# Attention and two mixers on one core: pairs 2 and 3 load into the buffers of pairs 0 and 1

## The chip, the cores and the metric

One core of a Trainium2 chip runs the whole program in one launch. The metric is the device time of one execution, in microseconds (us), as the median of several runs. Lower is better.

## What is computed

Three blocks follow each other. The first is attention over four batches of eight heads, 576 positions and 64 values a head: a pooled part (queries, keys and values averaged over groups of four positions, full softmax over 144 positions, result repeated four times) plus a local part (softmax over keys at most three positions away).

```python
q_d, k_d, v_d = (t.reshape(B, H, S // 4, 4, D).mean(axis=3) for t in (q, k, v))
out_up = np.repeat(sm_attn(q_d, k_d, v_d), 4, axis=2)
mask = np.abs(pos[:, None] - pos[None, :]) < 4
out_local = softmax(where(mask, q @ k.T / sqrt(D), -1e9)) @ v
x = merge_heads(out_up + out_local)                       # 4 x 576 x 512
# mixer 1
u = x + (relu(x.T @ w_tok1) @ w_tok2).T
x = u + relu(u @ w_ch1) @ w_ch2
# mixer 2
theta = x @ w_theta
u = x + w_tok_r @ (x * cos(theta)) + w_tok_i @ (x * sin(theta))
out = u + relu(u @ w_ch)
```

## The kernel before, in words

The sixteen pairs of heads (four a batch) are numbered 0 to 15, and two pairs make a quad, numbered 0 to 7. The queries and keys of a pair come in one DMA of 128 x 1164 float32 (582 KB, a tile named qk). The work is cut into small steps, Python generators, each advanced by one `yield` at a time:

- `P<n>` (`load_pair`, L375) allocates the qk tile of pair n and issues its DMA on SP. `W<n>` (`load_values`, L382) issues four DMAs for the local values (vw), `V<Q>` (`pool_values`, L391) one DMA of 650 KB for the values of quad Q to be pooled (vd), and then three POOL additions (L398 to L404).
- `K<n>` (`pool_pair`, L413) adds groups of four positions of qk on VectorE (DVE) in two instructions (L421, L422). The two pairs of a quad share one tile qkd.
- `F<Q>` (`quad_front`, L425) is the pooled attention of a quad: scores sd (L434, L443), maxima mxd (L452, L460), exponentials pd on ScalarE (ACT, L468, L473), a transpose pdt (L477, L482), the product od (L493 to L500), its normalisation ods (L504 to L507), a store of ods to DRAM (L510, L511), and a load back as xu, each row repeated (L516, L519). SP waits for the store to land before it issues the load.
- `L<n>` (`pair_local`, L522) is the local attention of a pair: scores s (L530, L533; L315 are matmuls of zeros ahead of the first four pairs), mx and pbuf on DVE (L545, L546), an exponential (L553), a transpose pt (L558), a copy plt (L561, L562), the product o (L568), and x on DVE (L577 to L582).
- `A<n>` (`add_pooled`, L590) adds xu to x, `T`, `E`, `U` are the token mixing, and `G0` to `G6` convert the int64 words of w_tok1 and w_tok2 into two float32r parts each (`converted`, L166: two ACT instructions L199 and L201, three DVE L203 to L215, one POOL L219, then L221 and L223). Tiles named raw and ww belong to these.

A table of step names, `ORDER` (L33 to L84), sets in which order the steps are advanced, and so the order of the instructions on each engine's queue, up to the end of mixer 1. `tc.manual_schedule` (L1131) records that order as it stands; a wait on one instruction holds up all that is queued behind it on its engine. Behind the table, mixer 2 (`stage_z`, `stage_y`, `stage_out`) is put in order by the framework's own scheduler.

The qk tiles come from a pool with four rotating buffers (L377), so that the order of the `P` steps decides which buffer a pair gets: pairs 0, 1, 4, 2 take the four fresh ones, pair 3 takes that of pair 0 and pair 5 that of pair 1. A DMA into a used buffer waits on SP until the readers of the old contents (`K` on DVE, the L533 matmuls on PE) are done. Score and transpose tiles in PSUM come from another pool with two buffers in turn (`wide`, L293), so that each waits for the last reader of the one before last.

Of the kernel before, what the change touches and what calls it, by code (L numbers as in the profile page):

```python
# [12 lines left out]
F32 = mybir.dt.float32  # L13
# [17 lines left out]
FIRST = 1  # L31
ROWS = ((8, 9), (0, 2), (4, 6), (2, 3))
ORDER = """  # L33
G3 P0 G2 I*2 P1 G3 P4 G3 V0 P2 G3 K0 G3 G2 I G2 I L0*2 P3 K1 F0 W1 L0 F0 L1 L0 G3 F0 V0 L1*2 V0 L2 W0 G1 G0 G6 V1 G2
K2 V0 G2 F0 L1 F0 L2 K3 K4 L0 F0 L0 L2 L1 G2 F1 L2 L1 L0 F0 F1 G1*2 F1 V1 F0 P5 F0 W3 L0 F1 G5 G0 L1 G0 F1 K5 G6 F2 L1
G0 P6 W2 G5 G6 L3 V1 F2 V1 L3 G6 F2 F1 L3 G1 G4 F1 L2 P7 L5 L2 L5 F1 G1 L3 A0 V2 X0 A1 T0 L3 G1 L5 G0 L3 T0 G0 L2 G2
F1 G4 F2 G5 T0 K6 T0 V2 X2 L2 G6 W5 F2 K7 V2 L4*2 E0.0*2 T0 L4 V3 V2 A2 L3 E0.1 L5 G4 L4 W4 L5 G6 L5 G4 L3 X2 F3 G5 P8
P9 A3 G4 F2 G5 E0.1 T1 G4 G5 T0 F2 V3 L4 F3 F2 T0 L4 V3 X2 F3 L6 V3 L6 X7 T0 P11 L6 X2 X0 F3 K8 U0.0 L6 T0 X2 X0 U0.0
F3 L4 U0.0 V4 K9 F2 F3 X0 L6 L4 L6 T1 F4 U0.1 X0 F3 T1 L5 U0.1 X0 T1 U0.1 F4 X7 X4 V4 F3 T1 X7 F4 W6 L5 X7 E1.1 F4
E1.0 E1.1 L8 V4 L8 X7 E1.0 X1 A4 F4 T1 P10 A5 T1 X2 T2 L8 T1 U1.0*2 T2 T1 U1.0 X1 F3 L7 X7 L7 T2 X1 T2 X4 X5 K10 X1 L8  # L40
L6 U1.1*2 L7 T2 E2.0 U1.1 W7 X4 L7 V4 X1 L7 F4 W9 L7 L6 X4 E2.1 E2.0 C0 E2.1 T2 X1 L8 K11 X5 L7 T2 X5 L8 W8 L9*2 L7 X5
P13 T2 P12 L9 L10 C0 A6 F5 X4 C0 U2.0 L10 U2.0 X5 U2.0 C0 X3 F5 X6 F4 F5 C0 A7 F4 L10 T3 X4 F5 L9 V5 T3 H0.1 L8 U2.1
F5 T2 H0.1 H0.0 K12 T3 L9 U2.1 X5 C0 L9 U2.1 K13 F4 X6*2 L10 T3 X3 W13 H0.0 X6 H0.2 F6 E3.0*2 V5 P14 T3 F6 V5 H0.2 F6
C0 V6 V5 L8 X3 E3.1 L9 H0.3 F5 E3.1 X3 W10 L9 F6 X3 F5 L10 V6 A9 T3 F5 T3 V6 U3.0 L10 K14 T3 V6 U3.0 X6 U3.0 T3 H0.3
# [43 lines left out]
LOWER, WIDE = 2, 2  # L88
MIX = 384
NMIX = 6  # L90
WARM = [24] + [12] * 3 + [0] * 12
DEEP = [4, 4]

B, H, S, D = 4, 8, 576, 64
# [20 lines left out]
def kernel(  # L115
# [172 lines left out]
    sb1 = actx.enter_context(tc.tile_pool(name="a1", bufs=1))  # L288
    sb2 = actx.enter_context(tc.tile_pool(name="a2", bufs=2))
# [3 lines left out]
    def wide(name):  # L293
        return big.tile([128, 2, 512], F32, tag="big", name=name)
# [17 lines left out]
    def warm(out, k):  # L312

        for _ in range(k):
            pe.matmul(out, zero[:, 0:128], zero[:, 0 : out.shape[-1]], start=True, stop=True)  # L315
# [4 lines left out]
    def step(name, gen):  # L320
        gens[name] = gen
# [52 lines left out]

    def load_pair(n):  # L375
        b, p4 = divmod(n, 4)
        qk = sb2.tile([128, 2, S + 6], F32, tag="qk", name=f"qk_{b}_{p4}", bufs=4)  # L377
        sp.dma_start(qk, qkT[b, p4])
        loaded[n] = qk
        yield  # L380
# [141 lines left out]
    def pair_local(n):  # L522
# [4 lines left out]
        s = wide(f"s_{at}")  # L527
        warm(s[:, 0, 192:512], WARM[n])
        for j in range(2):
# [419 lines left out]
    def lazily(f):  # L949
        yield from f()  # L950
# [190 lines left out]
    sb1 = ctx.enter_context(tc.tile_pool(name="c1p", reuse_waits="tile", bufs=1))  # L1141
    sb2 = ctx.enter_context(tc.tile_pool(name="c2p", reuse_waits="tile", bufs=2))
# [93 lines left out]
    T0, T1 = slice(0, HALF), slice(HALF, S)  # L1236
# [221 lines left out]
```

## Time and profile before

| what | value |
| --- | --- |
| median of 3 runs | 679.75 us (679.57 to 682.46) |
| profiled execution, its own time | 679.18 us |
| span of that execution, first to last instruction | 677.4 us |
| PE busy in the span | 655.6 us (97%) |
| DVE busy in the span | 519.8 us (77%) |
| ACT busy in the span | 321.1 us (47%) |
| POOL busy in the span | 100.1 us (15%) |
| chain that ended last, by engine | PE 84%, DMA 5%, DVE 5%, SP's queue 2%, ACT 2%, issue 1% |

The span and the busy times come from one profiled execution, whose own time lies 0.57 us under the median of the runs. What lies around the span is 1.78 us. PE is the engine with the most work; the windows below show in which stretches it is idle.

### The profile page before, as it was taken

How to read it: one execution, taken by the hardware profiler on the slowest of the kernel's cores; microseconds unless marked ns; L12 is line 12 of the kernel's file. 1: busy time of each engine (PE TensorE's matmuls, PEld its weight loads, DVE VectorE, ACT ScalarE, POOL GpSimd, SP SyncE). 2: the span in 40 equal slices, each digit the busy share in tenths (PEclk: the TensorE clock that was granted, in tenths of full speed). 3: DMA queues.
4: the chain of work that ended last, by engine and by line, in shares of the span. 5: the costliest groups of instructions: out<-in, count | busy, mean ns of one | idle time of the engine just before them, and what ended most of it. 6: DMA issues, size and time to landing. Idle time of an engine off the chain costs nothing.

```text
span 677.4 us, 17394 instructions
## 1 busy us (share of the span) xinstructions
PE 655.6 (97%) x7320; PEld 625.6 (92%) x7320; DVE 519.8 (77%) x952; ACT 321.1 (47%) x632; POOL 100.1 (15%) x92
## 2 busy tenths in 40 slices
PE   7779889999999999999999999999999999999997
PEld 4658879989999999999999999999999998998997
DVE  5989988697542888998987867677898748847837
ACT  3566758355342564535434523154647227427311
POOL 3224222415000423300101200012000000000000
PEclk8889999999999999999999999999999999999999
DMA  8797877757343685527263762699510330140202
GB/s 294 235 300 236 269 248 250 254 184 233 105 147 126 221 294 187 202 65 214 57 195 128 206 142 85 236 323 277 141 63 0 106 121 1 62 142 1 71 1 70
DMA packets 93021, 109.93 MB, mean 162 GB/s; under 512 B 46880, under 2 KB 69536, under 8 KB 92944
## 3 DMA queue, kind: packets, MB, share of 16 engines
q1 hardware_dynamic: 92080, 106.08, 49.4%
q0 software_dynamic: 864, 2.75, 1.1%
q8 instruction: 57, 0.93, 0.6%
q14 instruction: 20, 0.16, 0.1%
HBM read 79.13 MB, written 29.69 MB: 161 GB/s over the span
## 4 chain that ended last, share of the span: by engine, by line
PE 84%; DMA 5%; DVE 5%; SPq 2%; ACT 2%; issue 1%; DVEq 0%; ACTq 0%
PE y L157 6%; PE y L158 6%; PE y L159 6%; PE c L158 4%; PE c L157 4%; PE c L159 4%; PE c L699 4%; PE c L702 4%; PE c L700 4%; PE c_p L902 3%; PE c_p L905 3%; PE c_p L903 3%; PE th L158 2%; PE th L159 2%; PE th L157 2%; DMA qk<-qkT 2%
## 5 line engine op out<-in xcount | busy, mean ns | idle before, releaser
L158 PE MATMUL y<-wrl,zh 128*128 128x288 f32 x256 | 74.9, 296 | 0.0
L157 PE MATMUL y<-wrh,zh 128*128 128x288 f32 x256 | 74.8, 296 | 0.0
L159 PE MATMUL y<-wrh,zl 128*128 128x288 f32 x256 | 71.9, 295 | 0.0
L219 POOL TENSOR_TENSOR ww<-ww,raw 128x512 int32<-128x512 int32 (+2 forms) x30 | 41.0, 1373 | 160.1 <-DMA raw<-w_ch 52.9
L157 PEld LDWEIGHTS y<-wrh,zh 128*128 128x128 f32 x256 | 48.0, 188 | 0.0
L158 PEld LDWEIGHTS y<-wrl,zh 128*128 128x128 f32 x256 | 48.0, 188 | 0.0
L159 PEld LDWEIGHTS y<-wrh,zl 128*128 128x128 f32 x256 | 46.9, 188 | 0.0
L219 POOL TENSOR_TENSOR raw<-raw 128x512 int32<-128x512 int32 (+2 forms) x16 | 20.4, 1275 | 133.5 <-DVE raw L215 57.6
L1231 DVE TENSOR_TENSOR cx<-y,cx 128x288 f32<-128x288 f32 x32 | 14.6, 456 | 32.3 <-PE y L159 31.8
L151 ACT CAST cuh<-cx 128x288 fp32r<-128x288 f32 (+1 forms) x16 | 8.8, 553 | 59.6 <-DVE cx L1231 59.6
L199 ACT ACTIVATE ww<-raw 128x512 f32<-128x512 f32 (+2 forms) x30 | 19.5, 649 | 27.4 <-DVE c1l L223 9.5
L157 PE MATMUL th<-thh,cxh 128*128 128x512 f32 (+1 forms) x92 | 31.6, 343 | 0.0
L158 PE MATMUL th<-thl,cxh 128*128 128x512 f32 (+1 forms) x92 | 31.6, 343 | 0.0
L159 PE MATMUL th<-thh,cxl 128*128 128x512 f32 (+1 forms) x92 | 31.1, 343 | 0.0
L921 DVE SCALAR_TENSOR_TENSOR g<-c,g 128x384 fp32r<-128x384 f32 x40 | 21.1, 549 | 12.8 <-ACT g L918 12.8
L918 ACT ACTIVATE g<-c 128x384 fp32r<-128x384 f32 x40 | 19.2, 490 | 24.4 <-PE c L159 24.4
L201 ACT ACTIVATE raw<-raw 128x512 int32<-128x512 uint32 (+3 forms) x46 | 29.5, 641 | 0.0
L929 DVE TENSOR_TENSOR ut<-c,ut 128x384 f32<-128x384 f32 x32 | 17.1, 550 | 9.9 <-PE c L702 9.9
L568 PE MATMUL o<-vw,plt 38*32 38x65 f32 x1280 | 18.0, 231 | 3.8 <-issue 3.1
L157 PE MATMUL t<-w2h,h 128*128 128x256 f32 (+1 forms) x64 | 21.5, 337 | 0.0
L157 PE MATMUL c<-uh,c1h 128*128 128x384 f32 x64 | 21.4, 334 | 0.0
L159 PE MATMUL c<-uh,c1l 128*128 128x384 f32 x64 | 21.4, 334 | 0.0
(390 smaller groups left out, 2256.7 us busy)
## 6 DMA issues: line engine op xcount, KB each, us to landing
raw<-w_ch SPq DMA_DIRECT2D x27, 512.0 KB
qk<-qkT SPq DMA_DIRECT2D x16, 582.0 KB
xT<-ut SPq DMA_DIRECT2D x12, 768.0 KB
vd<-vtok SPq DMA_DIRECT2D x8, 650.0 KB
vw<-vloc SPq DMA_DIRECT2D x32, 146.2 KB
uT<-us SPq DMA_DIRECT2D x16, 288.0 KB
ut<-uT SPq DMA_DIRECT2D x6, 768.0 KB
ut<-xT SPq DMA_DIRECT2D x6, 768.0 KB
```

The costliest lines, as they stand in the source:

```text
L157: pe.matmul(out, lh, rh, start=start, stop=False, skip_group_check=again)
L158: pe.matmul(out, lh, rl, start=False, stop=False, skip_group_check=again)
L159: pe.matmul(out, ll, rh, start=False, stop=stop, skip_group_check=again)
L201: act.activation(f, words[:, :, 0], AF.Copy, scale=2.0**-29)
L219: pool.tensor_tensor(out=w.bitcast(I32), in0=w.bitcast(I32), in1=f, op=ALU.add)
L699: pe.matmul(ps[:, 0:MIX], h[:, cb % 2, d], h1, start=cb == cbs[0], stop=False)
L700: pe.matmul(ps[:, 0:MIX], l[:, cb % 2, d], h1, start=False, stop=False)
L702: pe.matmul(ps[:, 0:MIX], weight[cb // 2][2][:, cb % 2, d], h2, start=False, stop=cb == cbs[-1])
L902: pe.matmul(ps[:, 0:MIX], h[:, cb % 2, d], h1, start=cb == cbs[0], stop=False)
L903: pe.matmul(ps[:, 0:MIX], l[:, cb % 2, d], h1, start=False, stop=False)
L905: pe.matmul(ps[:, 0:MIX], weight[cb // 2][2][:, cb % 2, d], h2, start=False, stop=cb == cbs[-1])
L921: dve.scalar_tensor_tensor(out=h2, in0=ps, scalar=0.0, in1=h1.bitcast(F32), op0=ALU.max, op1=ALU.subtract)
```

## The change

The qk tiles no longer rotate. A tuple `QK` names for each pair one of four buffers that are allocated apart, so that pairs 2 and 3 load into the buffers of pairs 0 and 1, and pairs 4 and 5 get the two fresh ones. `ORDER` is rewritten in its first eight lines: `P4`, `P5`, `K4`, `K5`, the front of quad 2 (`F2`) and the load of `V1` stand later, `W0` and two weight loads earlier. One line is added, so that all lines of the changed kernel behind L90 have a number one higher.

```diff
@@ -31,14 +31,14 @@
 ORDER = """
-G3 P0 G2 I*2 P1 G3 P4 G3 V0 P2 G3 K0 G3 G2 I G2 I L0*2 P3 K1 F0 W1 L0 F0 L1 L0 G3 F0 V0 L1*2 V0 L2 W0 G1 G0 G6 V1 G2
...
+G3 P0 G2 I*2 P1 G3*2 V0 G3 K0 G3 G2 I G2 I L0*2 P2 W0 G1 K1 F0 L0 F0 L1 L0 G3 F0 V0 L1 P3 G0 W1 L1 V0 L2 G2 K2 V0 G2
...
@@ -88,6 +88,7 @@
 LOWER, WIDE = 2, 2
 MIX = 384
 NMIX = 6
+QK = (0, 1, 0, 1, 2, 3, 0, 1, 3, 2, 3, 0, 2, 1, 3, 0)
 WARM = [24] + [12] * 3 + [0] * 12
 DEEP = [4, 4]
 
@@ -374,7 +375,7 @@
 
     def load_pair(n):
         b, p4 = divmod(n, 4)
-        qk = sb2.tile([128, 2, S + 6], F32, tag="qk", name=f"qk_{b}_{p4}", bufs=4)
+        qk = sb1.tile([128, 2, S + 6], F32, tag=f"qk{QK[n]}", name=f"qk_{b}_{p4}")
         sp.dma_start(qk, qkT[b, p4])
         loaded[n] = qk
         yield
```

**First place: SP's queue behind the load of pair 1.** Before, from that load on (qk_1, a name that drops the batch; the second qk row is pair 4, the third and fourth are pairs 2 and 3):

```order
L378 DMA qk_1_148<-qkT 128x1164
L378 DMA qk_0_152<-qkT 128x1164
L396 DMA vd_0_157<-vtok 128x1300
L378 DMA qk_2_159<-qkT 128x1164
L378 DMA qk_3_240<-qkT 128x1164
L387 DMA vw_1_266<-vloc 32x1170 x2
L387 DMA vw_1_266<-vloc 6x1170 x2
L387 DMA vw_0_364<-vloc 32x1170 x2
```

Now, from the same load on (the qk rows are pairs 1, 2 and 3):

```order
L379 DMA qk_1_148<-qkT 128x1164
L397 DMA vd_0_155<-vtok 128x1300
L379 DMA qk_2_236<-qkT 128x1164
L388 DMA vw_0_238<-vloc 32x1170 x2
L388 DMA vw_0_238<-vloc 6x1170 x2
L188 DMA raw_243<-w_tok 128x2x256
L379 DMA qk_3_342<-qkT 128x1164
L188 DMA raw_344<-w_tok 128x2x256
L388 DMA vw_1_346<-vloc 32x1170 x2
```

Pair 4 has left this place, the vw of pair 0 comes ahead of that of pair 1, and pairs 2 and 3, which now wait for the readers of pairs 0 and 1, stand ahead of vw and weight loads.

**Second place: SP's queue from the second vd to the vw of pair 3.** Before (the qk row is pair 5):

```order
L187 DMA raw_373<-w_tok 128x288
L396 DMA vd_1_375<-vtok 128x1300
L510 DMA od_0_57<-ods_0_567 4x32x256
L511 DMA ot_0_65<-ods_0_567 4x32x64
L378 DMA qk_1_589<-qkT 128x1164
L516 DMA xu_0_591<-od_0_57 128x1x1024
L519 DMA xu_0_591<-ot_0_65 64x1x256 x2
L387 DMA vw_3_595<-vloc 32x1170 x2
L387 DMA vw_3_595<-vloc 6x1170 x2
```

Now (the qk rows are pairs 4 and 5):

```order
L511 DMA od_0_57<-ods_0_557 4x32x256
L512 DMA ot_0_65<-ods_0_557 4x32x64
L397 DMA vd_1_578<-vtok 128x1300
L517 DMA xu_0_580<-od_0_57 128x1x1024
L520 DMA xu_0_580<-ot_0_65 64x1x256 x2
L379 DMA qk_0_585<-qkT 128x1164
L379 DMA qk_1_587<-qkT 128x1164
L188 DMA raw_589<-w_tok 128x288
L388 DMA vw_3_591<-vloc 32x1170 x2
L388 DMA vw_3_591<-vloc 6x1170 x2
L188 DMA raw_615<-w_tok 128x288
```

The vd of quad 1 has moved behind the store of quad 0 (od, ot), pairs 4 and 5 and one weight load behind the load of xu, and the vw of pair 3 and the last weight load behind all of these.

**Third place: DVE from the pooling of pair 5 to the maxima of pair 3.** Before (qa_1 is pair 5; the pooling of pair 4 stands 19 rows earlier, between those of pair 3 and mx_2):

```order
L421 TENSOR_TENSOR qa_1_670<-qk_1_589 128x576
L422 TENSOR_TENSOR qkd_0_446<-qa_1_670 128x288
L577 TENSOR_SCALAR rl_1_697<-o_1_623 128x10
L578 RECIPROCAL rl_1_697<-rl_1_697 128x10
L582 TENSOR_TENSOR x_0_603<-o_1_623,rl_1_697 128x2x5x64
L203 TENSOR_SCALAR ww_673<-ww_673 128x288
L206 TENSOR_SCALAR ww_673<-ww_673 128x288
L215 SCALAR_TENSOR_TENSOR ww_673<-raw_373,ww_673 128x288
L452 TENSOR_REDUCE mxd_0_732<-sd_0_676 128x4
L460 TENSOR_REDUCE mxd_0_732<-sd_0_676 64x1 x2
L545 TENSOR_REDUCE mx_3_816<-s_3_715 128x10
L546 TENSOR_TENSOR pbuf_120<-s_3_715,mx_3_816 128x2x5x38
```

Now (qa_0 and qa_1 are pairs 4 and 5):

```order
L578 TENSOR_SCALAR rl_1_669<-o_1_619 128x10
L579 RECIPROCAL rl_1_669<-rl_1_669 128x10
L583 TENSOR_TENSOR x_0_599<-o_1_619,rl_1_669 128x2x5x64
L422 TENSOR_TENSOR qa_0_674<-qk_0_585 128x576
L423 TENSOR_TENSOR qkd_0_673<-qa_0_674 128x288
L422 TENSOR_TENSOR qa_1_677<-qk_1_587 128x576
L423 TENSOR_TENSOR qkd_0_673<-qa_1_677 128x288
L204 TENSOR_SCALAR ww_666<-ww_666 128x288
L207 TENSOR_SCALAR ww_666<-ww_666 128x288
L216 SCALAR_TENSOR_TENSOR ww_666<-raw_589,ww_666 128x288
L546 TENSOR_REDUCE mx_3_783<-s_3_694 128x10
L547 TENSOR_TENSOR pbuf_120<-s_3_694,mx_3_783 128x2x5x38
```

The pooling of both pairs stands behind the x of pair 1 now, and the maxima of quad 2 (mxd_0) have left; they come after the xl of quad 0, with the six exponentials of that quad on ACT later in the same way. On PE the scores sd of quad 2 have moved from behind the o of pair 1 to behind the pt of pair 3.

Behind the table, in mixer 2, the framework's scheduler puts some matmuls of `stage_y`, and DVE and ACT instructions beside them, in another order than before. Their numbers and shapes are the same.

## Rows read from the trace of the kernel before

**Rows 1.** Windows of the whole core: us, busy per engine (count), granted clock, DMA.

```profile
0.00:50.00 50.00, 37.92 (x1045) 27.48 (x1045) 38.53 (x76) 26.90 (x67) 15.95 (x21) 0.90 0.84 277
50.00:100.00 50.00, 45.66 (x1410) 39.96 (x1409) 45.65 (x87) 32.86 (x75) 17.00 (x14) 1.00 0.80 253
100.00:150.00 50.00, 49.04 (x965) 44.73 (x966) 41.33 (x79) 29.47 (x71) 11.89 (x12) 1.00 0.68 226
...
500.00:550.00 50.00, 50.00 (x344) 48.08 (x343) 40.62 (x74) 22.88 (x38) 0.00 (x0) 1.00 0.28 94
```

**Rows 2.** PE's waits from 150 to 450 us: total, times, longest.

```profile
PE p_a L157 <- ACT p_p L866: 0.3, 1, 0.3
```

**Rows 3.** Chain of waits, first 50 us: start, us, what.

```profile
3.53 5.99 DMA qk<-qkT
...
23.12 3.81 DMA od<-ods
...
32.42 2.65 DMA raw<-w_tok
...
36.05 1.20 ACT pd L468 x4
...
45.41 1.26 PE pdt L477 x5
...
47.68 0.51 PE t L157
```

**Rows 4.** Timeline of SP: start, us, issue (the length holds its waits).

```profile
4.95 4.19 SPq L378 DMA_DIRECT2D qk<-qkT  x2
...
18.89 0.38 SPq L396 DMA_DIRECT2D vd<-vtok  x1
...
27.00 0.61 SPq L516 DMA_DIRECT2D xu<-od  x1
...
29.59 2.79 SPq L387 DMA_DIRECT2D vw<-vloc  x4
```

**Rows 5.** Windows of five us, columns as in the first group.

```profile
5.00:10.00 5.00, 2.69 (x110) 1.74 (x107) 3.29 (x7) 1.32 (x4) 0.80 (x1) 1.00 1.00 353
...
45.00:50.00 5.00, 5.00 (x61) 3.88 (x49) 4.71 (x8) 1.92 (x6) 2.81 (x3) 0.66 0.93 301
```

**Rows 6.** Timeline of PE: start, us, instruction, in brackets idle before and releaser.

```profile
14.98 0.91 PE L533 MATMUL s<-qk 64*32 64x38 f32 x80
...
29.00 1.60 PE L568 MATMUL o<-vw,plt 38*32 38x65 f32 x79
...
37.94 0.77 PE L558 MATMUL pt<-fixed,pbuf 128*128 128x128 f32 x5 [0.89 <-ACT pd L473]
```

**Rows 7.** Timeline of DVE, 18 to 44 us.

```profile
18.25 0.76 DVE L421 TENSOR_TENSOR qa<-qk 128x576 f32<-128x576 f32 x1
...
19.54 0.76 DVE L421 TENSOR_TENSOR qa<-qk 128x576 f32<-128x576 f32 x1
20.33 0.46 DVE L422 TENSOR_TENSOR qkd<-qa 128x288 f32<-128x288 f32 x1
...
23.83 0.76 DVE L452 TENSOR_REDUCE mxd<-sd 128x4 f32<-128x576 f32 x1 [0.73 <-PE sd L443]
...
30.30 1.44 DVE L422 TENSOR_TENSOR qkd<-qa 128x288 f32<-128x288 f32 x1
...
32.10 0.82 DVE L582 TENSOR_TENSOR x<-o,rl 128x640 f32<-128x640 f32 x1
...
36.42 0.55 DVE L546 TENSOR_TENSOR pbuf<-s,mx 128x380 f32<-128x380 f32 x1
...
41.94 1.48 DVE L606 TENSOR_TENSOR xl<-x,xh 128x1280 fp32r<-128x1280 f32 x1
```

**Rows 8.** Timeline of ACT at 35 us.

```profile
35.09 0.48 ACT L199 ACTIVATE ww<-raw 128x288 f32<-128x288 f32 x1 [4.25 <-DMA raw<-w_tok]
```

**Rows 9.** Timeline of POOL at 30 us.

```profile
29.73 1.69 POOL L219 TENSOR_TENSOR raw<-raw 128x512 int32<-128x512 int32 x1 [1.77 <-PE pdt L482]
```

More of the change, by code (lines that the diff above doesn't have):

```diff
@@ L33 @@
 ORDER = """
-G3 P0 G2 I*2 P1 G3 P4 G3 V0 P2 G3 K0 G3 G2 I G2 I L0*2 P3 K1 F0 W1 L0 F0 L1 L0 G3 F0 V0 L1*2 V0 L2 W0 G1 G0 G6 V1 G2
[L35 to L41, printed above, removed]
+G3 P0 G2 I*2 P1 G3*2 V0 G3 K0 G3 G2 I G2 I L0*2 P2 W0 G1 K1 F0 L0 F0 L1 L0 G3 F0 V0 L1 P3 G0 W1 L1 V0 L2 G2 K2 V0 G2
+F0 L1 F0 L2 K3 L0 F0 L0 L2 L1 G2 F1 L2 L1 L0 F0 F1 G1*2 F1 F0 V1 F0 V1 P4 P5 G6 W3 L0 F1 G5 G0 L1 G0 F1 G6 L1 K4 K5 G0
+P6 W2 G5 G6 L3 V1*2 L3 G6 F1 L3 G1 G4 F1 L2 P7 L5 L2 L5 F1 G1 L3 A0 V2 X0 A1 T0 L3 F2 G1 L5 G0 L3 T0 F2 G0 L2 G2 F1 G4
+F2 G5 T0 F2 K6 T0 V2 X2 L2 G6 W5 F2 K7 V2 L4*2 E0.0*2 T0 L4 V3 V2 A2 L3 E0.1 L5 G4 L4 W4 L5 G6 L5 G4 L3 X2 F3 G5 P8 P9
+A3 G4 F2 G5 E0.1 T1 G4 G5 T0 F2 V3 L4 F3 F2 T0 L4 V3 X2 F3 L6 V3 L6 X7 T0 P11 L6 X2 X0 F3 K8 U0.0 L6 T0 X2 X0 U0.0 F3
+L4 U0.0 V4 K9 F2 F3 X0 L6 L4 L6 T1 F4 U0.1 X0 F3 T1 L5 U0.1 X0 T1 U0.1 F4 X7 X4 V4 F3 T1 X7 F4 W6 L5 X7 E1.1 F4 E1.0
+E1.1 L8 V4 L8 X7 E1.0 X1 A4 F4 T1 P10 A5 T1 X2 T2 L8 T1 U1.0*2 T2 T1 U1.0 X1 F3 L7 X7 L7 T2 X1 T2 X4 X5 K10 X1 L8 L6
+U1.1*2 L7 T2 E2.0 U1.1 W7 X4 L7 V4 X1 L7 F4 W9 L7 L6 X4 E2.1 E2.0 C0 E2.1 T2 X1 L8 K11 X5 L7 T2 X5 L8 W8 L9*2 L7 X5
 P13 T2 P12 L9 L10 C0 A6 F5 X4 C0 U2.0 L10 U2.0 X5 U2.0 C0 X3 F5 X6 F4 F5 C0 A7 F4 L10 T3 X4 F5 L9 V5 T3 H0.1 L8 U2.1
```

## Prediction, made before the changed kernel was run

> **What bounds the kernel now.** I read the windows of the whole core first [rows 1]. In the first 50 us PE is busy for 37.92, in the next for 45.66, then 49.04, and from there on all of the time (the window from 500 us stands for it); between 150 and 450 us PE waits once, for 0.3 us [rows 2]. So an edit ahead of 150 us is worth what it takes from the 17.4 us of PE idle time there (12.1 + 4.3 + 1.0), and a delay that PE takes over is seen at the end in full. The chain of waits [rows 3] shows what ends last in the stretch of the change: the q and k of pair 1 (3.53 to 9.52 us), the round trip of od through DRAM (3.81), a weight load (2.65), and then the exponentials pd of quad 2, the transpose pdt and the first matmul t of the token mixing at 47.68. Between these it runs on DVE, whose timeline has hardly a gap there [rows 7]; the one of 0.73 us ahead of mxd is the only one in these rows. The reader should see in them that DVE pools pairs 3 and 4 (18.25, 19.54) without a wait: those loads are early. The timeline of SP [rows 4] shows the DMAs' places, the five-us windows [rows 5] the rate of the DMA engines when they are full, 353 GB/s, and the clock of 0.66 from 45 to 50 us, a mean of the two levels (1.2 and 2.4 GHz).
>
> **The price of a load.** I need it three times and the trace has it only for other places. The weight load (128 x 288 int64, 288 KB) took 2.65 us from issue to landing in a short queue [rows 3]; a qk (582 KB, 596,000 bytes) adds 0.85 us at 353 GB/s: 3.5 us. The other end is pair 1's 5.99 us in a full queue. I take 3.5 where the queue is short, which it is behind the moved loads.
>
> **The sum, step by step.**
>
> 1. *Pair 4 leaves the head of SP's queue.* vd and the vw are served some 1.7 us earlier (596,000 bytes at 353 GB/s). Nobody on the chain waits for them: 0.
>
> 2. *Pair 2 waits for pair 0's readers.* Pair 3 waited for the same readers before, and that issue ended at 9.14 [rows 4]. Landed by 12.6, at 5.99 by 15.1; DVE wants it at 17.0 (18.25 less the 1.25 of one pooling, below): 0 from both ends. The vw and weights queued behind it on SP were held up to 17 us and more before.
>
> 3. *Pair 3 waits for the scores of pair 1.* These end at 15.89 [rows 6], so it lands at 19.4 and DVE waits 1.15 us at 18.25 (at 5.99: 3.6). Pair 4's pooling, 19.54 to 20.79, is gone from here: -1.25. Together -0.1; I write 0. So od is issued at 23.1 as before (25.5 at the other end). mxd behind it had 0.73 us to spare [rows 7].
>
> 4. *od goes into an emptier queue.* Before, the vd issued at 18.89 and pair 5 lay around it. Now vd goes out behind od and pair 5 behind xu. Bounds 2.65 and 3.81; I take 2.65, as nothing large is ahead: xu is issued at 25.8, not at 27.0. The xu loads hold SP for 2.6 us (27.0 to 29.59 [rows 4]), up to 28.4; pairs 4, 5 and the weights take three issues of 0.38; vw comes at 29.6, as before: 0 for all behind. vd at 24.3 is landed by about 28.4 (3.5 and 0.2 for its larger size), and its first POOL addition ends some 2 us later, near where POOL had its next work (29.73 [rows 9]); od of quad 1 is wanted by DVE only behind pbuf of pair 3, at 37: 0.
>
> 5. *Pairs 4 and 5 are pooled behind x of pair 1.* The o of pair 1 ends at 30.60 [rows 6]. Its x ended at 32.92, 1.2 us behind a pooling that ended at 31.74 [rows 7]; with nothing in front it ends at 31.8. Pair 4, issued at 28.4, lands at 31.9 and is pooled to 33.15; pair 5 lands 1.7 us later, 33.6, and is pooled to 34.85; the weights land another 0.84 later, 34.4, and ACT's 0.48 us [rows 8] make them ready at 34.9. Three DVE instructions of this conversion (some 1.2 us), then mx and pbuf (1.15, at 0.55 us and a step between): pbuf of pair 3 ends at 37.25, where it ended at 36.97 [rows 7]: **+0.3**, although the maxima of quad 2 no longer stand there.
>
> One row needs a choice here. Pair 5's second instruction took 1.44 us, pair 4's 0.46 [rows 7], and beside the long one POOL ran an addition of 1.69 us [rows 9]. I take 0.46, since POOL's next additions should be over by 33.6. The Trainium skill, SBUF — State Buffer, section Who interferes with whom, says that a VectorE instruction with two SBUF inputs contends with a GpSimd instruction that reads SBUF; the two rows agree. By that rule 0.46 holds if POOL is quiet then; were the 1.44 the instruction's own, 1 us would be added.
>
> 6. *The front of quad 2 goes behind pt of pair 3.* Before, pt of pair 2 waited 0.89 us for pd [rows 6], and pd for an ACT queue that stood for 4.25 us on the weight load [rows 8]. Both waits leave pt. plt behind it still waits for that last weight load on ACT. This load is issued when it was, but behind pair 5, weights and vw, and lands at about 36.3 (34.4, 1.0 for 355,000 bytes of vw, 0.84), not at 35.07; two ACT instructions later plt starts at 37.2, where it started at 38.7 at the earliest (37.94 + 0.77). So ACT and PE are 1.5 us early, DVE 0.3 late, and xl of quad 0 ends between 0.5 earlier and 0.3 later than 43.42 [rows 7]. Now the maxima of quad 2 come behind xl: 0.76 and two of some 0.3, to 44.3 or 45.1. Then pd: 1.9 us from 36.05 to the pt that it released at 37.94 [rows 3, 6], and 0.2 ahead for scaling: 46.4 or 47.2. pdt took 2.27 us (45.41 to 47.68 [rows 3]) in the slow stretch; at the full clock I estimate 1.2. The first matmul of the token mixing starts between 47.6 and 49.5, against 47.68: **0 to +1.8**, middle +0.9.
>
> 7. *Up to the end.* DVE has 4.35 us and PE 4.34 us idle from 50 to 100 us [rows 1], mostly waits for each other, so I let half of the 0.9 be absorbed: **+0.5**. In mixer 2 the scheduler's other order costs 0 as long as PE has no wait, which the window from 500 us shows. If it opens a gap, I bound it by 1 us, two of DVE's short instructions (0.55) per batch in one batch.
>
> The profiled execution took 679.18 us, so the sum is 679.7; against the median of 679.75 it is 680.25. I forecast **680.0 us: no change**. About 0.5% (3.4 us) is what a measurement of this kernel can tell from no change.
>
> **Rivals.**
>
> *Slower: the loads that were early collide.* Some 1.5 MB (pairs 4 and 5, weights) leave the quiet stretch around 18 us for the one behind xu, where vd, xu, two qk, weights and vw queue up in turn. If pairs 4 and 5 pay 5.99 us instead of 3.5, all of step 5 is 2.5 us later: pbuf at 39.75, +2.8. Quad 2's maxima, 1.4 us, stay behind it, and the PE that stands idle meanwhile runs pdt at the low clock: +4.2 at the token mixing, some 684 us at the end. It decides from the point at which DVE starts on pair 5 later than about 35.5. For it: the DMA engines' share is 0.84 over the first 50 us [rows 1], and 0.93 from 45 to 50 [rows 5]. Against it: the emptier queue before 23 us, which lets od, vd and xu through early. The Trainium skill, DMA: Bandwidth & Descriptors, section Rules for kernel authors, says to issue a DMA early, compute, and wait late; by it this rival would be the result, and the absence of a wait ahead of pairs 3 and 4 in rows 7 bears it out as far as the kernel before goes. 13%.
>
> *Faster: the waits on ACT were the bound.* Then pt and plt, 1.5 us early, pull the rest along, the wait of 0.89 us is gone for good and pdt runs at the full clock (1.1 us): 3.5 us in all, 676.2. For it: PE's 12.1 us of idle time in the first 50 us. Against it: DVE runs through, and gets none of its work taken away, only moved. 9%.
>
> *The moves cancel* (no landing is late, quad 2's maxima delay nothing): -0.5 to +0.5 us, 679.5. That is inside my forecast's band.
>
> **Chances and range.** My forecast with the last case has 78%, faster 9%, slower 13%. Within the forecast the bounds are -1.0 (od and the landings at their short ends, full clock) and +2.4 (step 3 at 5.99 us, no absorption). For 8 in 10 the range reaches a little into both rivals: 677.3 to 682.9.
>
> **What would show it.** Right: DVE waits about a us ahead of pair 3's pooling at 19.4; xu is issued near 26; pairs 4 and 5 are pooled between 32 and 35 with 0.46 us for the second instruction; pt of pair 2 shows no wait for pd; the first t matmul stands at 47.6 to 49.5; PE runs through from 150 us. Wrong: DVE waits 2 us or more for pair 4 or 5 (slower), the t matmul starts before 46 (faster), or PE has waits in mixer 2.

## The result and the profile after

| | median | runs | lowest to highest |
| --- | --- | --- | --- |
| before | 680.96 us | 13 | 675.66 to 683.92 |
| after | 684.82 us | 13 | 683.32 to 689.59 |

The ratio is 1.007 [1.0047 to 1.0092]: the changed kernel is slower by 0.7%, some 4.8 us by the ratio (the medians differ by 3.9). The forecast of 680.0 us (677.3 to 682.9) and of no change was wrong; the time is that of the rival to which I had given 13%, some 684 us.

The profiled execution of after took 689.59 us, the slowest of its 13; that of before, 679.18, lies under its median. The two spans, 687.8 and 677.4 us, thus differ by 10.4, more than twice what the ratio says. PE is busy for 659.4 us of the new span: 3.8 more than the 655.6 before, for the same instructions, and idle for 28.4 where it was idle for 21.8. Nearly all of these 6.6 us lie in the first 150 us (16.0 + 5.0 + 2.8 = 23.8 idle, 17.4 before [rows 1]). Windows of after, columns as in [rows 1]:

```profile
0.00:50.00 50.00, 34.02 (x1007) 25.03 (x1008) 34.29 (x69) 25.61 (x63) 14.30 (x20) 0.85 0.82 262
50.00:100.00 50.00, 45.05 (x1222) 39.27 (x1221) 47.16 (x88) 32.23 (x75) 16.32 (x15) 0.94 0.71 225
100.00:150.00 50.00, 47.17 (x999) 43.02 (x987) 35.55 (x66) 25.59 (x59) 11.50 (x12) 0.93 0.73 239
500.00:550.00 50.00, 50.00 (x344) 48.10 (x343) 44.00 (x78) 26.19 (x46) 0.00 (x0) 1.00 0.15 47
...
20.00:25.00 5.00, 2.95 (x137) 2.34 (x125) 3.96 (x12) 2.49 (x6) 0.00 (x0) 1.00 0.10 26
25.00:30.00 5.00, 2.93 (x103) 2.28 (x104) 4.38 (x11) 4.22 (x11) 1.14 (x1) 0.84 0.81 278
30.00:35.00 5.00, 5.00 (x153) 3.55 (x152) 2.20 (x4) 0.00 (x0) 3.15 (x4) 0.81 0.98 343
35.00:40.00 5.00, 0.75 (x7) 0.35 (x5) 3.58 (x10) 2.27 (x6) 1.26 (x2) 0.87 1.05 276
40.00:45.00 5.00, 3.60 (x121) 2.83 (x123) 4.87 (x7) 3.79 (x8) 0.79 (x1) 0.50 0.98 281
45.00:50.00 5.00, 2.60 (x100) 2.31 (x89) 4.31 (x8) 4.18 (x13) 1.82 (x2) 0.50 0.92 325
50.00:55.00 5.00, 5.00 (x36) 4.14 (x34) 4.48 (x8) 1.57 (x4) 0.99 (x2) 0.50 0.94 268
```

The row to start from is the one at 20 us: the DMA engines are busy for 0.10 of it. The same window of before:

```profile
20.00:25.00 5.00, 3.98 (x121) 3.15 (x122) 4.02 (x11) 3.14 (x7) 0.00 (x0) 1.00 0.87 310
```

That is 1.55 MB moved before (5 us at 310 GB/s) and 0.13 MB now. The 1.4 MB come back from 30 us on, where the share is 0.92 and more. Behind them DVE and ACT have gaps, PE has 0.75 us of work from 35 to 40, and from 40 to 55 us it is granted 0.50, the lower of its two levels. The timeline of SP of after:

```profile
13.48 0.36 SPq L379 DMA_DIRECT2D qk<-qkT  x1
...
24.18 0.44 SPq L397 DMA_DIRECT2D vd<-vtok  x1
26.75 0.60 SPq L517 DMA_DIRECT2D xu<-od  x1
...
28.72 1.06 SPq L379 DMA_DIRECT2D qk<-qkT  x2
29.82 0.43 SPq L188 DMA_DIRECT2D raw<-w_tok  x1
```

And the timelines of DVE, ACT and PE of after, with the idle time before an instruction and its releaser in brackets:

```profile
19.28 0.78 DVE L422 TENSOR_TENSOR qa<-qk 128x576 f32<-128x576 f32 x1 [3.49 <-DMA qk<-qkT]
...
33.52 0.76 DVE L422 TENSOR_TENSOR qa<-qk 128x576 f32<-128x576 f32 x1 [2.50 <-DMA qk<-qkT]
34.32 0.46 DVE L423 TENSOR_TENSOR qkd<-qa 128x288 f32<-128x288 f32 x1
35.60 0.76 DVE L422 TENSOR_TENSOR qa<-qk 128x576 f32<-128x576 f32 x1 [0.83 <-DMA qk<-qkT]
36.40 0.46 DVE L423 TENSOR_TENSOR qkd<-qa 128x288 f32<-128x288 f32 x1
37.46 0.31 DVE L204 TENSOR_SCALAR ww<-ww 128x288 f32<-128x288 f32 x1 [0.60 <-ACT ww L200]
...
39.10 0.55 DVE L547 TENSOR_TENSOR pbuf<-s,mx 128x380 f32<-128x380 f32 x1
```

```profile
36.97 0.46 ACT L200 ACTIVATE ww<-raw 128x288 f32<-128x288 f32 x1 [7.53 <-DMA raw<-w_tok]
...
38.55 0.46 ACT L200 ACTIVATE ww<-raw 128x288 f32<-128x288 f32 x1 [0.77 <-DMA raw<-w_tok]
...
39.27 0.57 ACT L562 COPY plt<-pt 128x512 f32<-128x512 f32 x1
```

```profile
34.70 0.77 PE L559 MATMUL pt<-fixed,pbuf 128*128 128x128 f32 x5
...
39.72 0.50 PE L531 MATMUL s<-fixed,id 128*128 128x190 bf16 x2 [4.25 <-DVE pbuf L547]
...
51.65 0.58 PE L158 MATMUL t<-xh,w1h 128*128 128x256 f32 x1
```

Read from the top: pair 4 is awaited for 2.50 us and pair 5, 2.08 us behind it, for 0.83 more; the weight issued behind them lands last of the three, and ACT stands on it for 7.53 us. The pbuf of pair 3 ends at 39.65 (36.97 before [rows 7]); PE has waited 4.25 us for it. The first t matmul of the token mixing starts 4.0 us late (51.65, in the chain 51.72; before 47.68 [rows 3]). The chain that ended last shows the lengths of these loads in after:

```profile
13.48 5.71 DMA qk<-qkT
...
22.88 3.85 DMA od<-ods
...
29.82 7.13 DMA raw<-w_tok
...
49.38 1.33 PE pdt L478 x5
...
51.72 0.51 PE t L158
```

### The profile page after: what moved, and what is told of

It is laid out like the page before. It is cut to its first block, busy times and chain, and to the rows that moved or that the text cites. A ratio compares the mean times of both kernels' runs of the same rounds, so it can differ in the third digit from the quotient of the medians.

```text
span 687.8 us, 17391 instructions
## 1 busy us (share of the span) xinstructions
PE 659.4 (96%) x7320; PEld 629.8 (92%) x7320; DVE 521.5 (76%) x952; ACT 321.1 (47%) x632; POOL 98.5 (14%) x92
## 4 chain that ended last, share of the span: by engine, by line
PE 84%; DMA 7%; DVE 5%; ACT 2%; SPq 1%; issue 1%; DVEq 0%; ACTq 0%
PE y L159 6%; PE y L158 6%; PE y L160 6%; PE c L158 4%; PE c L160 4%; PE c L159 4%; PE c L700 4%; PE c L703 4%; PE c L701 4%; PE c_p L906 3%; PE c_p L904 3%; PE c_p L903 3%; PE th L158 2%; PE th L160 2%; PE th L159 2%; PE t L158 2%
## 5 line engine op out<-in xcount | busy, mean ns | idle before, releaser
L200 ACT ACTIVATE ww<-raw 128x512 f32<-128x512 f32 (+2 forms) x30 | 19.4, 646 | 31.1 <-DVE c1l L224 9.4
L159 PE MATMUL c<-ul,c1h 128*128 128x384 f32 x64 | 21.4, 334 | 0.0
```

What stands on the lines that cost most here:

```text
L159: pe.matmul(out, lh, rl, start=False, stop=False, skip_group_check=again)
```

## The experiments

All ratios are to the kernel before, run on the same chip beside it, with the 95% interval; before's median lay between 680.96 and 683.4 us from set to set, so that ratios are compared, not times. The edits move tokens in `ORDER`; the diffs show the pieces of its lines that differ. Nothing of the computation is left out.

### Undoing parts of the change

My theory after the result: the loads of pairs 4 and 5 are late, so issuing them early again, with all else as changed, gives the time back. The rival: the late front of quad 2 costs.

Both loads early, into their fresh buffers, behind the vw of pair 1:

```diff
-W0 G1 K1 F0 L0 F0 L1 L0 G3 F0 V0 L1 P3 G0 W1 L1
+W0 G1 K1 F0 L0 F0 L1 L0 G3 F0 V0 L1 P3 G0 W1 P4 P5 L1
...
-F0 V1 F0 V1 P4 P5 G6 W3
+F0 V1 F0 V1 G6 W3
```

> The changed kernel with the loads of pairs 4 and 5 issued ahead of the store of quad 0 (behind the vw of pair 1, near 17 us) instead of behind xu; SP's order alone changes. Theory of late loads: what the change lost is that two qk and a weight load queue up behind xu (DVE stood 2.50 + 0.83 + 0.60 us for them). Then these 3.9 us go: pbuf of pair 3 ends near 36 instead of 39.65 us, the first t matmul stands near 48 instead of 51.7, and the ratio to the kernel before is 0.998 to 1.002 (679.5 to 682.3 us). Theory of the late front: the maxima and exponentials of quad 2 behind xl are what PE waits for; then t comes at 50 us or later and the ratio stays at 1.005 or more (684 us).

Front of quad 2 at its old place, behind the pooling of pair 5:

```diff
-L1 K4 K5 G0
+L1 K4 K5 F2 G0
...
-L3 V1*2 L3 G6 F1
+L3 V1 F2 V1 L3 G6 F2 F1
```

> The changed kernel with the front of quad 2 back at its old place (scores behind the pooling of pair 5, maxima and exponentials ahead of those of pair 3); the loads stay late. Theory of late loads: the waits of DVE for pairs 4 and 5 and for the weight stay (3 to 4 us in all), 1.4 us of maxima come on top of them ahead of pbuf of pair 3 (near 41 us), and are gone from behind xl; t matmul at 49.5 to 52, ratio 1.004 to 1.009. Theory of the late front: t matmul at 48, ratio 0.998 to 1.002.

Both edits at once (no other line differs):

> The changed kernel with both: loads of pairs 4 and 5 early and the front of quad 2 at its old place. What is left of the change is the wait of pair 3 for the buffer of pair 1, vd of quad 1 behind the store of quad 0, and the order of the weight loads. Both theories: 0.997 to 1.002 and t matmul near 48 us. If it stays at 1.004 or more, the loss lies in what is left: pair 3 (DVE waits 3.5 us for it) or vd.

The front alone, late in the kernel before (`F2` moved as in the change):

```diff
-K5 G6 F2 L1
+K5 G6 L1
...
-L3 V1 F2 V1 L3 G6 F2 F1
+L3 V1*2 L3 G6 F1
...
-T0 L3 G1 L5 G0 L3 T0 G0
+T0 L3 F2 G1 L5 G0 L3 T0 F2 G0
...
-G5 T0 K6
+G5 T0 F2 K6
```

> The kernel before with the front of quad 2 alone moved as the change does (scores behind pt of pair 3, maxima behind xl, exponentials behind these); all loads as before. Theory of late loads: the move of the front costs little: pbuf of pair 3 some 1.4 us earlier (35.6 us), t matmul at 46.5 to 48.5, ratio 0.997 to 1.002. Theory of the late front: t matmul at 50 us or later, ratio 1.004 to 1.008.

| kernel | ratio |
| --- | --- |
| e1, loads of 4 and 5 early | 1.0051 [1.0023 to 1.0078] |
| e2, front early | 1.0111 [1.0065 to 1.0157] |
| e3, both | 1.0057 [1.0030 to 1.0084] |
| e4, before with the front late | 1.0003 [0.9974 to 1.0032] |

The rival is out: a late front costs nothing that these runs can tell, and with late loads an early one is not better but, by the middles, worse (e2). But e1 gives back only 0.2% by its middle; the theory as I stated it fell too. Its profile shows the two waits gone, and others in their place. The window at 20 us, DVE and ACT of e1:

```profile
20.00:25.00 5.00, 2.79 (x112) 2.22 (x102) 3.99 (x9) 2.52 (x7) 0.00 (x0) 1.00 1.03 293
...
20.01 0.76 DVE L422 TENSOR_TENSOR qa<-qk 128x576 f32<-128x576 f32 x1 [3.82 <-DMA qk<-qkT]
...
32.80 0.75 DVE L422 TENSOR_TENSOR qa<-qk 128x576 f32<-128x576 f32 x1
...
34.51 1.06 DVE L422 TENSOR_TENSOR qa<-qk 128x576 f32<-128x576 f32 x1
...
37.66 0.55 DVE L547 TENSOR_TENSOR pbuf<-s,mx 128x380 f32<-128x380 f32 x1
42.58 0.56 DVE L547 TENSOR_TENSOR pbuf<-s,mx 128x380 f32<-128x380 f32 x1 [0.74 <-ACT w1h L222]
...
35.49 0.49 ACT L200 ACTIVATE ww<-raw 128x288 f32<-128x288 f32 x1 [4.33 <-DMA raw<-w_tok]
```

Pairs 4 and 5 are there in time, the first weight behind xu still is not: ACT stands for 4.33 us on it, and DVE waits for ACT at 42.58. The length of that wait alone is not the loss, since ACT stood for 4.25 us on a weight in the kernel before, too [rows 8]. And the DMA engines are full from 20 to 25 us here (1.03), so that the idle window of after is gone without the loss being gone.

### One part at a time, in either kernel

Open now: the late pair 3 (3.5 us of waiting), the late vd, or the buffers. e5 takes e1 and gives pairs 2 and 3 fresh buffers, issued early; pairs 4 and 5 then go into those of pairs 0 and 1:

```diff
-QK = (0, 1, 0, 1, 2, 3, 0, 1, 3, 2, 3, 0, 2, 1, 3, 0)
+QK = (0, 1, 2, 3, 0, 1, 2, 3, 1, 0, 1, 2, 0, 3, 1, 2)
...
+V0 P2 P3 G3 K0
```

> The run with early loads (e1_loads_early) with pairs 2 and 3 in the two fresh buffers and issued right behind the first vd, and pairs 4 and 5 in the buffers of pairs 0 and 1; SP's order and the buffers change, the order of the compute engines does not. Theory of the late pair 3: in e1_loads_early DVE stood 3.82 us for pair 3 (issue 13.89, landed 20.0) and that wait is what is left of the loss, 0.5%. Then the wait is under 0.5 us, od of quad 0 is issued 2 to 3 us earlier (near 21 us), and the ratio is 0.998 to 1.002. Theory that the loss lies elsewhere (vd of quad 1, pooling of pair 4 taken out of the early part of DVE, buffers of later pairs): 1.004 to 1.007 in spite of it.

Before with the tuple of buffers written out, pairs and order as they were:

```diff
+QK = (0, 1, 3, 0, 2, 1, 3, 0, 1, 2, 1, 3, 2, 0, 1, 3)
...
-        qk = sb2.tile([128, 2, S + 6], F32, tag="qk", name=f"qk_{b}_{p4}", bufs=4)
+        qk = sb1.tile([128, 2, S + 6], F32, tag=f"qk{QK[n]}", name=f"qk_{b}_{p4}")
```

> The kernel before with the buffers of pairs 6 to 15 chosen as the changed kernel chooses them (pair 6 takes that of pair 2, 7 that of 3, 8 of 5, 9 of 4 and so on); the order of all engines stays. If the waits of the later loads for other readers are part of the loss: ratio 1.003 to 1.006, and PE loses its time behind 60 us, not ahead of it. If not: 0.998 to 1.002.

Before with the vd of quad 1 behind the store of od:

```diff
-F1 V1 F0 P5 F0 W3
+F1 F0 V1 P5 F0 V1 W3
```

> The kernel before with the load of the values of quad 1 (vd) alone moved behind the store of quad 0, as the change has it. If late values are part of the loss (POOL's three additions end near 35 instead of 33 us and the od of quad 1 waits for them): ratio 1.002 to 1.005. If the od of quad 1, which stood at 35.7 us, is not held up: 0.998 to 1.002.

Before with pairs 2 and 3 in the buffers of 0 and 1 (the tuple of the change), their loads as late as there:

```diff
-V0 P2 G3 K0
+V0 G3 K0
...
-L0*2 P3 K1 F0 W1 L0 F0 L1 L0 G3 F0 V0 L1*2 V0
+L0*2 P2 K1 F0 W1 L0 F0 L1 L0 G3 F0 V0 L1 P3 L1 V0
```

> The kernel before with pairs 2 and 3 loaded into the buffers of pairs 0 and 1, pair 3 issued behind the scores of pair 1 and the vw of pair 1, pairs 4 and 5 in fresh buffers but at their old places; all compute engines in the old order. Theory of the late pair 3: DVE waits 2 to 3.5 us ahead of pair 3's pooling at 18.3 us, od of quad 0 is issued near 25 us, and the ratio is 1.003 to 1.006. If the loss lies elsewhere: 0.999 to 1.002 (DVE makes the wait good later).

| kernel | ratio |
| --- | --- |
| e5, e1 with pairs 2 and 3 in fresh buffers | 1.0085 [1.0050 to 1.0121] |
| e6, before, buffers named | 0.9977 [0.9952 to 1.0001] |
| e7, before, vd late | 1.0006 [0.9984 to 1.0029] |
| e8, before, pairs 2 and 3 late | 1.0008 [0.9980 to 1.0035] |

The e6 kernel came out as a control: the pool of before had already dealt out the same buffers, so only names and addresses differ, and every queue keeps its order. Its 0.9977 tells that 0.25% can't be read in these sets. e7 and e8 clear two suspects, although in e8 DVE waits 3.16 us for pair 3 at 19.44: the wait is real, its price nothing. e5 missed: with more loads early it is, by the middles, worse than e1. From 5 to 20 us the DMA share is 1.04 to 1.06 there, and PE stops three times without a releaser (the third time for 2.92 us, up to 48.61). The first two stops in PE of e5:

```profile
16.25 0.31 PE L534 MATMUL s<-qk 64*32 64x38 f32 x17 [2.18 <-issue]
...
25.38 0.26 PE L534 MATMUL s<-qk 64*32 64x38 f32 x4 [3.33 <-issue]
```

Next, the place of the pooling. e9 is e4 with `K4 K5` behind the x of pair 1: all compute engines in the order of after, all loads as in before.

```diff
-K3 K4 L0
+K3 L0
...
-F1 K5 G6 L1
+F1 G6 L1 K4 K5
```

> The kernel e4_before_front_late with the pooling of pairs 4 and 5 (four DVE instructions) moved behind x of pair 1, as the change has it: every compute engine is now in the order of the changed kernel, and all loads stand as before. Theory of the late pooling: pair 4's pooling (1.25 us) leaves a part of DVE's timeline that was otherwise idle and comes into the full one from 30 to 45 us; pbuf of pair 3 ends 1.2 us later or more and the ratio is 1.003 to 1.006, that of e1_loads_early (1.0051). Theory of the order of the loads (weights and vw around pair 3 and behind xu): the ratio stays at that of e4_before_front_late, 0.998 to 1.002.

e10 is e1 with the pooling where before has it:

```diff
-K3 L0
+K3 K4 L0
...
-F1 G6 L1 K4 K5 G0
+F1 K5 G6 L1 G0
```

> The kernel e1_loads_early with the pooling of pairs 4 and 5 back at its old places on DVE (pair 4 behind pair 3, pair 5 ahead of x of pair 1); all loads as in e1_loads_early. Theory of the late pooling: 0.999 to 1.003 instead of 1.0051. Theory of the order of the loads: 1.004 to 1.006 stays.

e11 is after with pair 4 (load and pooling) back at its old place, e12 the same with pair 5 too. The diff is that of e12 against e11:

```diff
-F1 F0 V1 F0 V1 P5 G6 W3 L0 F1 G5 G0 L1 G0 F1 G6 L1 K5 G0
+F1 F0 V1 P5 F0 V1 G6 W3 L0 F1 G5 G0 L1 G0 F1 K5 G6 L1 G0
```

> The changed kernel with pair 4 alone undone: its load back behind that of pair 1, its pooling back behind that of pair 3; pair 5, the front of quad 2, vd and the weights stay where the change puts them. Theory of the late loads and pooling together: two thirds of the loss go (582 KB less behind xu, 1.25 us less DVE behind 30 us): 1.001 to 1.004. Theory of the order of the loads: 1.005 to 1.007.

> The changed kernel with pairs 4 and 5 wholly undone: both loads and both poolings at their old places. What is left is all the rest of the change: the buffers of pairs 2 and 3 and the wait that comes with them, the front of quad 2 late, vd of quad 1 late, vw and weight loads in the new order. Theory that pairs 4 and 5 (load and pooling) are the whole loss: 0.998 to 1.002. Theory that the new order of vw, weights and pair 3 carries its own share (e11_pair4_early stayed at 1.0057): 1.003 to 1.006.

| kernel | ratio |
| --- | --- |
| e9, before, pooling and front late | 1.0038 [1.0017 to 1.0060] |
| e10, e1 with pooling early | 1.0090 [1.0057 to 1.0123] |
| e11, after, pair 4 undone | 1.0057 [1.0033 to 1.0082] |
| e12, after, pairs 4 and 5 undone | 1.0044 [1.0019 to 1.0069] |

e10 missed. In its profile pair 4, issued at 17.43 when the DMA share is 0.88 (15 to 20 us) and then 0.98 (20 to 25 us), is awaited in DVE's order, and od goes out only at 28.96:

```profile
25.37 0.76 DVE L422 TENSOR_TENSOR qa<-qk 128x576 f32<-128x576 f32 x1 [3.90 <-DMA qk<-qkT]
```

e12 says that even without any move of pairs 4 and 5 most of the loss stays, by the middles; e11, with pair 4 alone undone, says the same. e9 pointed at the pooling, so I split it. Pooling of pair 4 late, in before:

```diff
-K3 K4 L0
+K3 L0
...
-F1 K5 G6 F2 L1
+F1 K4 K5 G6 F2 L1
```

> The kernel before with the two pooling instructions of pair 4 alone moved, from behind those of pair 3 to ahead of those of pair 5; loads and all other engines as before. Theory of the late pooling of pair 4 (1.25 us of DVE from a part with slack into the full part): 1.002 to 1.004. If the loss of e9_before_pool_late (1.0038) came from pair 5: 0.998 to 1.001.

Pooling of pair 5 late (e15, against e4), and its load late too (e14, against e4, both lines):

```diff
-V1 F0 P5 F0 W3
+V1 F0 F0 P5 W3
...
-F1 K5 G6 L1
+F1 G6 L1 K5
```

> The kernel e4_before_front_late with the pooling of pair 5 alone moved behind x of pair 1, its load as before. The pooling stays in the full part of DVE's timeline, only behind three instructions (1.2 us) instead of ahead of them, which lets x of pair 1 be earlier: 0.998 to 1.001. If the loss of e9_before_pool_late came from pair 5: 1.003 to 1.005.

> The kernel e4_before_front_late with pair 5 alone as the change has it: load behind xu, pooling behind x of pair 1. Theory of the late load: DVE waits 2 to 4 us for pair 5 and the ratio is 1.003 to 1.007. If only the place of the pooling counts, it is that of e15_pool5_late.

| kernel | ratio |
| --- | --- |
| e13, before, `K4` just ahead of `K5` | 1.0022 [0.9996 to 1.0048] |
| e14, e4 with `P5` behind xu, `K5` behind x | 1.0029 [1.0002 to 1.0057] |
| e15, e4 with `K5` behind x | 1.0025 [0.9999 to 1.0051] |

None can be told from the others, and hardly from 1: this was a blind alley.

### The gap filled

The last set took up the idle stretch at 20 us as a whole. e17 is after with vd, the weight and pairs 4 and 5 issued behind the vw of pair 1. Only SP's order changes: compute engines and buffers are those of after.

```diff
-P3 G0 W1 L1
+P3 G0 W1 G6 V1 P4 P5 L1
...
-F1 F0 V1 F0 V1 P4 P5 G6 W3
+F1 F0 F0 V1 W3
```

> The changed kernel with all its late loads (pairs 4 and 5, vd of quad 1, the w_tok2 load) issued behind the vw of pair 1, near 17 us, where its DMA engines stand idle (0.10 from 20 to 25 us); compute engines as in the changed kernel. Theory that the loads left a gap and crowd behind xu: the 20 to 25 us window is filled (0.7 and more), nothing on DVE waits for a load from 28 to 40 us, and the ratio falls from 1.007 to what the place of the pooling costs alone, 1.002 to 1.005 (e9_before_pool_late: 1.0038). If the crowding costs nothing: 1.006 to 1.008 stays.

e16 is e4 with vw and weights in the order of the change:

```diff
-P3 K1 F0 W1 L0
+P3 W0 G1 K1 F0 L0
...
-V0 L1*2 V0 L2 W0 G1 G0 G6 V1 G2
+V0 L1 G0 W1 L1 V0 L2 V1 G2
...
-P5 F0 W3
+P5 F0 G6 W3
```

> The kernel e4_before_front_late with vw of pair 0 ahead of that of pair 1, two weight loads between them and the first w_tok2 load of this stretch behind xu, as the change has these; vd, all qk loads and all compute engines stay. Theory that the order of the weights carries the loss of e12_pairs_back (1.0044) by itself: 1.003 to 1.005. Theory that it needs the late vd, the late pair 3 and the late weight together, since each alone fits into the gap: 0.999 to 1.002.

e18 is before with the pooling late but the front early:

```diff
-K3 K4 L0
+K3 L0
...
-F1 K5 G6 F2 L1
+F1 G6 L1 K4 K5 F2
```

> The kernel before with the pooling of pairs 4 and 5 moved behind x of pair 1 and the front of quad 2 right behind it, ahead of the local attention of pair 3 (the compute order of e3_both); all loads as before. It is a second measure of the place of the pooling, with the maxima (1.4 us) behind it too: theory of the late pooling 1.004 to 1.008, and more than e9_before_pool_late; if the pooling's place is not what counts, 0.998 to 1.002.

| kernel | ratio |
| --- | --- |
| e17, after, four loads in the gap | 1.0001 [0.9978 to 1.0024] |
| e16, e4 with vw and weights as changed | 1.0050 [1.0023 to 1.0076] |
| e18, before, pooling late, front early | 1.0010 [0.9982 to 1.0037] |

e17 takes back the whole loss, and its interval lies clear of that of after (from 1.0047). Its window shows the gap filled:

```profile
20.00:25.00 5.00, 2.59 (x100) 2.01 (x89) 4.00 (x10) 2.33 (x6) 0.00 (x0) 1.00 1.01 335
```

and its timelines, DVE, POOL, ACT and PE in turn:

```profile
19.99 0.76 DVE L422 TENSOR_TENSOR qa<-qk 128x576 f32<-128x576 f32 x1 [4.07 <-DMA qk<-qkT]
...
32.62 1.24 DVE L422 TENSOR_TENSOR qa<-qk 128x576 f32<-128x576 f32 x1
33.89 0.76 DVE L423 TENSOR_TENSOR qkd<-qa 128x288 f32<-128x288 f32 x1
34.68 0.76 DVE L422 TENSOR_TENSOR qa<-qk 128x576 f32<-128x576 f32 x1
...
37.49 0.55 DVE L547 TENSOR_TENSOR pbuf<-s,mx 128x380 f32<-128x380 f32 x1
...
32.48 0.76 POOL L402 TENSOR_TENSOR vs<-vd 128x325 f32<-128x325 f32 x1
33.32 1.01 POOL L405 TENSOR_TENSOR vl<-vs,fixed 128x260 f32<-128x260 f32 x1
...
30.95 0.47 ACT L200 ACTIVATE ww<-raw 128x288 f32<-128x288 f32 x1
34.82 0.49 ACT L200 ACTIVATE ww<-raw 128x288 f32<-128x288 f32 x1 [3.03 <-DMA raw<-w_tok]
36.45 0.58 ACT L562 COPY plt<-pt 128x512 f32<-128x512 f32 x1 [0.77 <-PE pt L559]
...
50.03 0.58 PE L158 MATMUL t<-xh,w1h 128*128 128x256 f32 x1
```

Pair 3 is as late as in after (4.07 us of waiting), but nothing waits for pairs 4 and 5, and plt waits for PE, not for a weight. pbuf ends at 38.04, 1.61 us ahead of after, and t comes 1.62 ahead. The pooling of pair 4 stretches from 0.76 and 0.46 to 1.24 and 0.76 while POOL adds. I had expected 1.002 to 1.005, with the late pooling still to pay; so e9's 1.0038 falls as a verdict on the late pooling: e17 has the same order on every compute engine, e18 the same place of the pooling, and both lie at 1.001 or under.

So the loss lies in the order of SP's loads: e17 differs from after in nothing else. What the sets leave open is which of the four loads it was, and by what way it costs. A full window at 20 us is not enough: the DMA share there is 1.03 in e1 and 0.98 in e3 and e10, and all three keep the loss. Moving pairs 4 and 5 alone gives 1.0051 (e1); moving vd and the weight as well gives 1.0001; vd alone costs nothing in before (e7). Sorted afterwards, all nine kernels with the weight load behind xu (after, e1, e2, e3, e5, e10, e11, e12, e16) lie at 1.0044 or over, and all ten of the other order at 1.0038 or under. That points at the weight, but no run moved it alone. e16, with vd and all pairs loaded early, came out where its first theory had it (1.0050), but it also exchanges the vw; its profile shows stops of PE with no releaser (the longest 3.1 us), and e7 has six such stops by 48 us, 8.2 us in all, at 1.0006. Nor is the wait on ACT shown to be the way: in e3 ACT starts on the last weight of this stretch at 35.79 us, as early as in e4 (35.85), and the ratio is 1.0057 against 1.0003. No kernel was faster than the one before.

## Why the prediction was wrong

**The step that failed is the price of a load:** "I take 3.5 where the queue is short, which it is behind the moved loads." It was not short: the DMA share is 0.81 from 25 to 30 us and 0.98 from 30 to 35. Pair 4, issued at 28.72, was there at 33.5 and so took 4.8 us; pair 5 came at 35.6, and the weight behind them, 7.13 us on its way, at 36.95. 31.9, 33.6 and 34.4 were forecast. Pair 3 took 5.71 us. The bound of 5.99 from the full queue [rows 3] was near, and the idle engines at 20 us were my reason against it: loads not issued then were not spread out but met behind xu. That is where the forecast leaves after's trace, and e17, with the four loads early again, is back at 1.0001. How much of the 0.7% the pairs' part makes is not shown: e1 takes their waits away and stays at 1.0051.

**Steps 1 and 2** held: pair 2 was pooled without a wait at 14.55.

**Step 3**, pair 3: it landed at 19.2 (forecast 19.4), since it was issued 2.4 us earlier than I had worked out and took 2.2 us longer. od went out at 22.88 (forecast 23.1). The wait on DVE was 3.49 us, not 1.15, because DVE was ahead by then. Right in its result: e8 and e17 show such a wait at no cost.

**Step 4**, "od goes into an emptier queue": the queue was nearly empty (a share of 0.10 from 20 to 25 us) and the store still took 3.85 us, as in the full one (3.81 [rows 3], the store alone, which the prediction calls the round trip). xu was issued at 26.75, not 25.8, and with it all behind it 0.3 to 0.95 later. vd, too, took 4.7 us: issued at 24.18, awaited by POOL up to 28.86.

**Step 5**, +0.3 at pbuf of pair 3, was +2.7 (39.65, where 36.97 was before and 37.25 forecast): pair 5 2.0 us late, then 0.60 of waiting for the weight. That is the size of the rival, which put pbuf at 39.75 and pair 5 behind 35.5. The choice of 0.46 for the second pooling instruction was right in after.

**Step 6**: pt lost its wait for pd, as forecast. plt did not come at 37.2 but at 39.27, since ACT stood on both weights. And pdt, for which I had estimated 1.2 us at the full clock, took 2.3 (49.38 to 51.72 in the chain) at a granted 0.50. How t hangs on pbuf was mis-sized too. With the late front, t comes 12.0 to 12.6 us behind the end of the pbuf of pair 3, in e4 as in after; I had 10.4 to 12.3. DVE's pbuf and PE's t in e4:

```profile
36.69 0.55 DVE L546 TENSOR_TENSOR pbuf<-s,mx 128x380 f32<-128x380 f32 x1
...
49.86 0.58 PE L157 MATMUL t<-xh,w1h 128*128 128x256 f32 x1
```

**Step 7**, "I let half of the 0.9 be absorbed": e4 has pbuf as early as I forecast (37.24), t 2.2 us late, and a ratio of 1.0003 [0.9974 to 1.0032]: by the middle all of it was absorbed, not half. But what a late t costs can't be read off at all. The same matmul in e7, whose ratio is 1.0006:

```profile
50.96 0.58 PE L157 MATMUL t<-xh,w1h 128*128 128x256 f32 x1
```

That is 3.3 us later than before at no price, and e6, with the order of before on every queue, has t at 50.44; e3 has it at 49.89 and costs 0.57%. So the place of t moves by some 3 us from one profile to another without any change of order, and that after's 4.0 us at t stand beside 4.8 us at the end does not show that the one made the other. In after's profile PE loses another 2.5 us of busy time from 50 to 150 us (7.8 idle, 5.3 before), with the granted clock at 0.94 and 0.93 where it was 1.00 [rows 1]. One piece of this is a stop of 2.58 us with no releaser at 107.77; the others I did not trace, and this is the slowest execution of its 13.

Mixer 2's other order cost nothing: PE is busy for 449.9 of the 450 us from 200 to 650 us (449.7 before).

**The rival that came true** had in its favour that late loads are the cause, which e17 confirms, and it had the sizes in after's trace: +2.7 at pbuf (it said +2.8) and +4.0 at t (+4.2). It was too narrow in its price, which came from pairs 4 and 5 alone: e1 and e12 show that these alone are not it. And as no run shows that the end follows t one for one, that it named 684 us is in part luck. By the Trainium skill, DMA: Bandwidth & Descriptors, section Rules for kernel authors, a DMA is to be issued early and its semaphore waited for late; after and e17 agree (1.007 against 1.0001), e1 and e5, which issue loads early too, do not (1.0051 and 1.0085). I quoted it and gave it 13%, because I weighed the waits before and not the bytes per window.

## What to carry to other kernels

Before moving a load, add up what each five-us window of the DMA engines will move, before and after: in after the bytes that left an idle window came back behind it as waits, although every moved load seemed to have time. A window that is full again is no proof that the loss is gone (e1, e3, e10). Price a load that joins others by the measured time in a full queue, not by the one in a short queue, and look at each in-order queue that it stands in: a late weight holds ACT, and all that is queued there. But more loads early were no gain in e5, work that is moved ahead of its load waits in order and holds up what is behind it (e10), and a wait that shows in the profile (pair 3, 3 to 4 us) may cost nothing.

## What the runs showed of the hardware

- A small store took long without company: od, issued at 22.88 in after where the DMA share from 20 to 25 us was 0.10, took 3.85 us, against 3.81 in before, where it was 0.87. By the Trainium skill, DMA: Bandwidth & Descriptors, section Anatomy of one DMA — SWDGE (gpsimd) path, a transfer on that path costs about 2.0 us, most of it to confirm that the last byte has landed, plus its bytes at 436 GB/s; for od's 131,072 bytes (4 x 32 x 256 float32) that would be an estimate of 2.3 us. This store was issued from SP and not on that path, and measured longer.
- PE stopped for up to 3.3 us with no releaser ("issue") in e5 and 3.1 us in e16, where the DMA share was 1.02 and over from 5 to 20 us. Full DMA engines alone do not make such a stop: in e12, with a share of 1.00 to 1.04 in that stretch, PE has no such stop above 0.3 us there. What the stops have in common is their place: ahead of the last 17 score matmuls s of pair 0 and the last 4 of pair 1 in e5, e6, e7, e9, e13, e15, e16 and e18 alike (0.9 to 2.2 and 0.9 to 3.3 us). Their cause was not shown.
- Two kernels with the same order on every queue differed by 0.23% (e6, 0.9977 [0.9952 to 1.0001]), and executions of one kernel by 8 us (before, 675.66 to 683.92): less than half a per cent is not read from one set.
